# Window attention and a gated feed-forward block: the general path as loops, and row sums taken among the gate steps

## The chip, the core and the metric

The kernel runs on one core of a Trainium2 chip. The metric is the device time of one execution in microseconds; the median of several runs is compared.

## What is computed

```python
# q, k, v: (8 batches, 8 heads, 576 positions, 64), float32
scores = (q @ k^T) / 8                     # per batch and head
mask   = (rel >= 0) & (rel < 64)           # rel = query position - key position
attn   = softmax(where(mask, scores, -1e9))
x      = (attn @ v), heads side by side    # 4608 tokens x 512
g      = x @ w_gate                        # 512 x 1536
out    = (silu(g) * (x @ w_val)) @ w_out   # 1536 x 512; out 4608 x 512 float32
```

## The kernel before

The 4608 tokens are worked off as nine tiles of 512 (t = 0 to 8). Eight of them are the first 512 positions of one batch each; tile `LAST` = 7 gathers the last 64 positions of all eight batches. A tile goes through three stages.

- Attention. Scores of two head pairs at a time go to PSUM (L292). `weigh` (L307) turns them into exponentials on ScalarE, without taking a row maximum off first, and writes them to one of four tiles `eb`; VectorE multiplies by the mask (L313). Row sums come from matmuls with ones (L336), and their inverses from a logarithm and an exponential on ScalarE (L350, L353). The second product (L414) is scaled into `xT` (L430).
- Gate steps. Twelve steps m = 0 to 11 (`gate_value`, L473): eight 128x512 matmuls, four for the gate and four for the value; Silu on ScalarE (L466); the product on VectorE into `hT` (L467). The PSUM banks of both alternate between two.
- Projection. `hT` times `wo` (L482, L494), copies to SBUF (L502) and stores on SyncE's queue (L511, L513). The projection of tile t-1 is interleaved with the attention of tile t. In the last tile nothing follows it, and `project_last` splits the last 128 tokens into 384 and 128 columns (L535, L539, L540).

The order on each engine is the order of the program (`manual_schedule`); nothing reorders it.

Since no row maximum is taken off, the kernel checks that the exponentials stayed in range. 56 columns of `spread` hold row values: of tile 0 by `survey_first`, and of the later tiles as sums that ScalarE accumulates along with the exponentials of L307 (32 columns, `accum_out=extent()`, an extra instruction that reads the accumulator) and with those of L353 (16 columns). In the last tile, `survey` (L546, L547) compares all columns with a limit behind gate step 4, and `tally` (L551, L552) counts by a matmul the partitions that are in range, behind step 7, and casts the result to the integer `count`. Behind the last gate step each of the five engines loads `count` into a register (L961). At the very end they branch (L970): if the count is 128, and so it is with these inputs, they jump over the general path, which would compute everything again in a slower, safe way. The general path is unrolled: eight batches of eight heads of attention, then the feed-forward, all written out, with loads and stores on SyncE's queue. Between the second and third projection of the last tile a branch hint is given on every engine. Behind the jump each engine adds to its semaphores what the skipped code would have added (L970), and the end of the program (L998) waits for all semaphores, lets the engines meet, clears the semaphores and lets them meet again.

Of the kernel before, what the change touches and what calls it, by code (L numbers as in the profile page):

```python
# [8 lines left out]
P = 128  # L9
# [2 lines left out]
AF = mybir.ActivationFunctionType  # L12
ALU = mybir.AluOpType
PSUM = bass.MemoryType.PSUM
EVERY = tuple(
    getattr(mybir.EngineType, n) for n in ("PE", "SP", "DVE", "Activation", "Pool")
)


@with_exitstack  # L20
def kernel(
# [10 lines left out]
    nc = tc.nc  # L32
# [35 lines left out]
    spread = cst.tile([P, 6 * NT + 2], FP32, name="spread")  # L68
    within = cst.tile([P, 2], BF16, name="within")
    count = cst.tile([P, 1], mybir.dt.int32, name="count")  # L70
    floor = cst.tile([P, 1], FP32, name="floor")
    LEAST, MOST = 2.0 ** -60, 2.0 ** 30
    columns_used = [0]
# [229 lines left out]
    def weigh(t, w, h, s_ps):  # L303
        n = 1024 if t == LAST else 960
        E = eb[2 * w + h]
        flat = E[:].rearrange("r s z -> r (s z)")[:, 64:64 + n]
        nc.scalar.activation(  # L307
            flat, s_ps[:].rearrange("r a b -> r (a b)")[:, 0:n], AF.Exp, scale=0.125,
            accum_out=extent(),
        )  # L310

        def masked():
            nc.vector.tensor_mul(  # L313
                flat, flat, mask[:].rearrange("r j c e y -> r (j c e y)")[:, 0:n]
            )
# [237 lines left out]

    def general_attention(b):

        x_b = v12[:].rearrange("r g i h d -> r (g i h d)")[:, 0:4 * S]
        x_b = x_b.rearrange("r (c s) -> r c s", c=4)
        chunks = [(P * c, min(S, P * c + P)) for c in range(5)]
        set_exp()
        for hd in range(H):  # L560
            u, h = hd // 2, hd % 2
            wide = {}
            for n, (src, tag) in (("q", (q, "q")), ("k", (k, "k"))):
                f = stage.tile([P, 5, D], FP32, name=n + "_g", tag=tag)
                nc.sync.dma_start(f[:, 0:4], src[b, hd, 0:512].rearrange("(c r) d -> r c d", r=P))
                nc.sync.dma_start(f[0:64, 4], src[b, hd, 512:S])
                bf = epool.tile([P, 5, D], BF16, name=n + "_h", tag="both")
                nc.vector.tensor_copy(bf[:, 0:4], f[:, 0:4])
                nc.vector.tensor_copy(bf[0:64, 4], f[0:64, 4])
                tp = bank[4 if n == "q" else 5].bitcast(BF16)  # L570
                for c, (lo, hi) in enumerate(chunks):
                    nc.tensor.transpose(
                        tp[0:D, lo:hi], bf[0:hi - lo, c], identb[0:hi - lo, 0:hi - lo]
                    )
                wide[n] = att.tile([P, S], BF16, name=n + "_w", tag="qT")
                nc.vector.tensor_copy(wide[n][0:D], tp[0:D, 0:S])
            vf = stage.tile([P, 5, D], FP32, name="v_g", tag="v", bufs=1)
            nc.sync.dma_start(vf[:, 0], v[b, hd, 0:P])
            nc.sync.dma_start(vf[:, 1:5], v[b, hd, 64:S].rearrange("(c r) d -> r c d", r=P))
            vh = epool.tile([P, 5, D], BF16, name="v_h", tag="both")  # L580
            nc.vector.tensor_copy(vh[:], vf[:])
            for c, (lo, hi) in enumerate(chunks):
                nq, k0 = hi - lo, max(0, lo - 64)
                nk = hi - k0
                s_ps = bank[6][0:nq, 0:nk]
                nc.tensor.matmul(s_ps, wide["q"][0:D, lo:hi], wide["k"][0:D, k0:hi])
                w = fsb.tile([P, 512], FP32, name="w_g", tag="sg")
                s = w[0:nq, 0:nk]
                nc.scalar.activation(s, s_ps, AF.Copy, scale=0.125)
                for sign, base in ((1, lo - k0), (-1, 63 + k0 - lo)):  # L590
                    nc.gpsimd.affine_select(
                        out=s, in_=s, compare_op=ALU.is_ge, fill=-1e9,
                        base=base, pattern=[[-sign, nk]], channel_multiplier=sign,
                    )
                top, total = w[0:nq, 256:257], w[0:nq, 257:258]
                nc.vector.tensor_reduce(top, s, axis=mybir.AxisListType.X, op=ALU.max)
                nc.vector.tensor_scalar(top, top, -1.0, 0.0, op0=ALU.mult, op1=ALU.add)
                nc.scalar.activation(s, s, AF.Exp, bias=top, accum_out=total)
                nc.vector.tensor_scalar(total, total, 1.0, 1e-9, op0=ALU.mult, op1=ALU.add)
                nc.vector.reciprocal(total, total)  # L600
                e = epool.tile([P, 192], BF16, name="e_g", tag="e_g", bufs=1)
                nc.vector.tensor_scalar(e[0:nq, 0:nk], s, total, 0.0, op0=ALU.mult, op1=ALU.add)
                tp = bank[7].bitcast(BF16)
                pT = fsb.tile([P, 2, P], BF16, name="p_g", tag="p_g", bufs=1)
                parts = [(0, P)] + ([(P, nk)] if nk > P else [])
                for i, (j0, j1) in enumerate(parts):
                    nc.tensor.transpose(
                        tp[0:j1 - j0, P * i:P * i + nq], e[0:nq, j0:j1], identb[0:nq, 0:nq]
                    )
                    nc.vector.tensor_copy(  # L610
                        pT[0:j1 - j0, i, 0:nq], tp[0:j1 - j0, P * i:P * i + nq]
                    )
                o_ps = bank[4][half(h), 0:nq]
                for i, (j0, j1) in enumerate(parts):
                    nc.tensor.matmul(
                        o_ps, vh[0:j1 - j0, c + i], pT[0:j1 - j0, i, 0:nq],
                        start=i == 0, stop=i == len(parts) - 1,
                    )
                nc.vector.tensor_copy(x_b[half(h), u, lo:hi], o_ps)
        return x_b  # L620

    def general_ffn(b, x_b):

        set_silu()
        for lo, hi in ((0, 512), (512, S)):
            n = hi - lo
            h_b = hpool.tile([P, 12, 512], BF16, name="h_b", tag="hT")
            for m in range(12):
                for w, ps_ in ((wg, bank[4]), (wv, bank[5])):
                    for c in range(4):  # L630
                        nc.tensor.matmul(
                            ps_[:, 0:n], w[:, c, P * m:P * m + P], x_b[:, c, lo:hi],
                            start=c == 0, stop=c == 3,
                        )
                sg = fsb.tile([P, 512], FP32, name="sg", tag="sg")
                nc.scalar.activation(sg[:, 0:n], bank[4][:, 0:n], AF.Silu)
                nc.vector.tensor_mul(h_b[:, m, 0:n], sg[:, 0:n], bank[5][:, 0:n])
            for r0 in range(0, n, P):
                rows = min(P, n - r0)
                for c in range(12):  # L640
                    nc.tensor.matmul(
                        bank[6][0:rows], h_b[:, c, r0:r0 + rows], wo[:, c, :],
                        start=c == 0, stop=c == 11,
                    )
                os_ = fsb.tile([P, 512], FP32, name="os_", tag="os_", bufs=4)
                nc.vector.tensor_copy(os_[0:rows], bank[6][0:rows])
                at = S * b + lo + r0
                nc.sync.dma_start(out[at:at + rows], os_[0:rows])

    def set_exp():  # L650
        nc.scalar.preload_act_table_set("natural_log_exp_and_others")
# [80 lines left out]
        return lambda: log(inverse[0, u], bank[b]), lambda: invert(inverse[0, u])  # L732

    firsts = {}

    def survey_first(u):

# [166 lines left out]
    for t in range(1, NT):  # L904
# [45 lines left out]
        turns = (6, 7, 9, 10) if t == 1 else (1, 4, 7, 10)  # L950
        for m in range(12):
            gate_value(t, m)
            if t == NT - 1 and m == 4:
                survey()
            if t == NT - 1 and m == 7:
                tally()
            if m in turns and t + 1 < NT:
                turn(t + 1, turns.index(m))
            if (t, m) in late:
                turn_k(kT[2], k_l, late.index((t, m)))  # L960
# [9 lines left out]
    with tc.If(good < P, preferred_fallthrough_block=True, label="settled"):  # L970
        for b in range(8):
            x_b = general_attention(b)
            general_ffn(b, x_b)

# [1 line left out]
_INS = ['q', 'k', 'v', 'moe_w_gate', 'moe_w_val', 'moe_w_out']  # L976
# [26 lines left out]
```

## Time and profile before

| | |
|---|---|
| median of 3 runs | 326.08 us (326.05 to 326.44) |
| the profiled execution | 325.93 us, span 324.2 us, 1.73 us around it |
| granted TensorE clock | 0.998 |
| busy: TensorE, VectorE, ScalarE, GpSimd | 97%, 66%, 55%, 46% |
| last matmul issued | 318.16 us |
| instructions in the span | 8153 |

The profile is of one execution; times within it are in us from the start of the span. The engines are PE (TensorE matmuls), PEld (its weight loads), DVE (VectorE), ACT (ScalarE), POOL (GpSimd) and SP (SyncE); a q behind the name stands for the engine's sequencer, which runs branches, register loads, semaphore waits and DMA issues. q1 is the DMA queue of SyncE's transfers; q8 and q14 carry instructions.

### The profile page before, as it was taken

To read this page: it belongs to the slowest core of one execution; us is meant where nothing else is said; L and a number is where in the kernel's file an instruction comes from. 1 tells how busy PE (TensorE), PEld (TensorE's weight loads), DVE (VectorE), ACT (ScalarE), POOL (GpSimd) and SP (SyncE) were. 2 spreads that over 40 slices of the span, in tenths; PEclk is the share of its full clock that TensorE was granted. 3 is DMA by queue.
4 is the path that set the end of the run, shared out by engine and by line. 5 is a ranking of instruction groups with operands and counts; after the bars stand their busy time and mean duration, and the time that the engine had idled before them with its cause. 6 is when DMAs were issued, how large, how long until landed. Compare 5 with 4: busy or idle time off the path is not lost.

```text
span 324.2 us, 8153 instructions
## 1 busy us (share of the span) xinstructions
PE 314.4 (97%) x3267; PEld 158.4 (49%) x3298; DVE 213.7 (66%) x349; ACT 178.8 (55%) x295; POOL 147.7 (46%) x268
## 2 busy tenths in 40 slices
PE   8899999999999999999999999999999999999992
PEld 3544444445444644464445544554456444644441
DVE  4879846497576747685687658866785668654321
ACT  4967675348533873387337833693368434853300
POOL 4965656867567245742751099309665300000000
PEclk9999999999999999999999999999999999999999
DMA  7999999999599449974993379529997400020022
GB/s 238 207 196 198 207 144 234 198 191 140 120 189 198 49 114 177 195 76 106 161 197 40 87 114 117 54 64 144 188 175 92 107 0 2 10 93 32 2 69 71
DMA packets 83534, 40.50 MB, mean 125 GB/s; under 512 B 64160, under 2 KB 78752, under 8 KB 83488
## 3 DMA queue, kind: packets, MB, share of 16 engines
q0 software_dynamic: 51488, 22.59, 58.4%
q1 hardware_dynamic: 31456, 16.79, 22.9%
q8 instruction: 27, 0.44, 0.6%
q10 hardware_dynamic: 544, 0.52, 0.5%
q14 instruction: 19, 0.16, 0.2%
HBM read 53.02 MB, written 9.44 MB: 193 GB/s over the span
## 4 chain that ended last, share of the span: by engine, by line
PE 77%; DMA 14%; POOL 4%; issue 2%; DVE 1%; SPq 0%; POOLq 0%
PE one L473 45%; PE one L482 14%; PE one L494 11%; DMA wv<-in_moe_w_val_dram 3%; DMA wo<-in_moe_w_out_dram 3%; PE two L292 3%; DMA q_s<-in_q_dram 2%; PE two L414 2%; DMA wg<-in_moe_w_gate_dram 2%; DMA vb<-in_v_dram 2%; POOL k_s L141 1%; DMA q_f<-in_q_dram 1%; PE one L535 1%; POOL v L159 1%; PE one L336 1%
## 5 line engine op out<-in xcount | busy, mean ns | idle before, releaser
L466 ACT ACTIVATE sg<-one 128x512 f32<-128x512 f32 x107 | 63.9, 597 | 112.5 <-PE one L473 86.2
L467 DVE TENSOR_TENSOR hT<-sg,one 128x512 bf16<-128x512 f32 x107 | 74.0, 693 | 57.7 <-PE one L473 54.0
L473 PE MATMUL one<-xT,wv 128*128 128x512 bf16 x409 | 106.4, 379 | 1.0
L473 PE MATMUL one<-xT,wg 128*128 128x512 bf16 x405 | 104.7, 379 | 0.1
L141 POOL DMA_DIRECT2D k_s<-in_k_dram x112 | 60.4, 561 | 27.5 <-DMA q_s<-in_q_dram 14.3
L473 PEld LDWEIGHTS <-wv 128*128 128x128 bf16 x416 | 40.7, 98 | 49.4 <-issue 0.4
L473 PEld LDWEIGHTS <-wg 128*128 128x128 bf16 x416 | 40.6, 98 | 48.8
L482 PE MATMUL one<-wo,hT 128*128 128x512 bf16 x241 | 55.4, 379 | 0.7 <-issue 0.3
L937 POOL COPY past<-xT 128x1 bf16<-128x1 bf16 x8 | 1.5, 190 | 88.0 <-DVE xT L430 88.0
L494 PE MATMUL one<-wo,hT 64*64 64x512 bf16 x672 | 40.4, 376 | 0.0
L482 PEld LDWEIGHTS <-hT 128*128 128x128 bf16 x252 | 23.7, 98 | 29.4 <-issue 2.0
L232 DVE STREAM_TRANSPOSE kT<-k_s 128x512 bf16<-128x512 bf16 x28 | 36.1, 1288 | 0.5 <-DMA vb<-in_v_dram 0.5
L430 DVE TENSOR_TENSOR xT<-two,r 128x512 bf16<-128x512 f32 x34 | 21.2, 683 | 21.9 <-ACT r L353 21.9
L307 ACT ACTIVATE eb<-two 128x960 bf16<-128x960 f32 (+1 forms) x32 | 31.0, 973 | 3.8 <-PE two L292 3.7
L494 PEld LDWEIGHTS <-hT 64*64 64x64 bf16 x672 | 21.1, 107 | 11.3
L313 DVE TENSOR_TENSOR eb<-eb,mask 128x960 bf16<-128x960 bf16 (+1 forms) x32 | 20.9, 655 | 7.9 <-ACT eb L307 7.9
L222 DVE STREAM_TRANSPOSE qT<-q_s 128x512 bf16<-128x512 bf16 x32 | 22.3, 700 | 0.1
L353 ACT ACTIVATE r<-r 128x1024 f32<-128x1024 f32 (+1 forms) x20 | 19.2, 969 | 0.1
L318 DVE TENSOR_TENSOR both<-eb 128x512 bf16<-128x512 bf16 x32 | 13.6, 425 | 1.1
L106 POOL DMA_DIRECT2D q_s<-in_q_dram x24 | 13.0, 551 | 2.2 <-DMA v<-in_v_dram 1.2
L167 POOL DMA_DIRECT2D vb<-in_v_dram x16 | 11.1, 708 | 5.8 <-DMA wo<-in_moe_w_out_dram 3.6
L350 ACT ACTIVATE r<-one,floor 128x512 f32<-128x512 f32 x17 | 10.9, 683 | 3.5 <-PE one L336 3.5
(148 smaller groups left out, 265.3 us busy)
## 6 DMA issues: line engine op xcount, KB each, us to landing
k_s<-in_k_dram POOLq DMA_DIRECT2D x112, 56.0 KB, 5.0
q_s<-in_q_dram POOLq DMA_DIRECT2D x24, 248.0 KB, 6.2
v_f<-in_v_dram SPq DMA_DIRECT2D x40, 128.0 KB
wg<-in_moe_w_gate_dram POOLq DMA_DIRECT2D x5, 256.0 KB, 8.4
wv<-in_moe_w_val_dram POOLq DMA_DIRECT2D x5, 256.0 KB, 9.0
q_f<-in_q_dram SPq DMA_DIRECT2D x4, 256.0 KB
wo<-in_moe_w_out_dram POOLq DMA_DIRECT2D x2, 512.0 KB, 10.6
vb<-in_v_dram POOLq DMA_DIRECT2D x16, 64.0 KB, 6.3
```

The source lines that it names most:

```text
L141: nc.gpsimd.dma_start(k_s[p0:p0 + 32, g, :, 0:w], k[b, a:H:2, s:s + P].rearrange("u (r e) d -> r u (e d)", e=4) [:, :, 32 * c:32 * c + w],)
L222: nc.vector.transpose(queries[t][:, u, :].rearrange("r (e x) -> r e x", e=16), staged[t][0][:, u].rearrange("r (e d) -> r e d", d=D)[:, :, ...
L232: nc.vector.transpose(dst[:, u, :].rearrange("r (g x e) -> r g e x", g=4, e=4), k_s[:, :, u].rearrange("r g (e d) -> r g e d", d=D)[:, :, ...
L307: nc.scalar.activation(flat, s_ps[:].rearrange("r a b -> r (a b)")[:, 0:n], AF.Exp, scale=0.125, accum_out=extent(),)
L313: nc.vector.tensor_mul(flat, flat, mask[:].rearrange("r j c e y -> r (j c e y)")[:, 0:n])
L353: nc.scalar.activation(r, r, AF.Exp, scale=-1.0, **kept)
L430: nc.vector.tensor_mul(x, o_ps, r)
L466: nc.scalar.activation(sg[:], g_ps[:], AF.Silu)
L467: nc.vector.tensor_mul(hT[t][:, m, :], sg[:], v_ps[:])
L473: nc.tensor.matmul(ps[:], w[:, c, P * m:P * m + P], xT[t][:, c, :], start=(c == 0), stop=(c == 3),)
L482: nc.tensor.matmul(o_ps[:], hT[t][:, c, P * s:P * s + P], wo[:, c, :], start=(c == 0), stop=(c == 11),)
L494: nc.tensor.matmul(tiles[s][half(y)], hT[t][half(x), c, r0:r0 + 64], wo[half(x), c, :], start=not back and c == 0, stop=bool(back) and c = ...
```

## The change

The general path becomes two loops that run on the chip, one over 64 pairs of batch and head and one over eight batches; what attention makes goes between them through a scratch array in device memory, `x_all`. Its loads and stores are issued by ScalarE. Its largest body is 642 instructions (of one engine), its smallest 99. The branch hints are left out. The row sums of the 32 exponentials of the later tiles are no longer accumulated with them: `survey_later` takes them from the masked exponentials by a copy in place on ScalarE, behind gate steps 3, 5, 6 and 8 of the same tile. In the last tile the survey moves from behind step 4 to behind step 8, and the tally from behind step 7 to behind step 10.

```diff
@@ (constants)
-EVERY = tuple(
-    getattr(mybir.EngineType, n) for n in ("PE", "SP", "DVE", "Activation", "Pool")
-)
@@ (tiles)
+    scratch = ctx.enter_context(
+        tc.tile_pool(name="scratch", bufs=1, space=bass.MemoryType.DRAM)
+    )
+    x_all = scratch.tile([2 * H * 8 * D, S // 2], BF16, name="x_all")
@@ weigh
         nc.scalar.activation(
-            flat, s_ps[:].rearrange("r a b -> r (a b)")[:, 0:n], AF.Exp, scale=0.125,
-            accum_out=extent(),
+            flat, s_ps[:].rearrange("r a b -> r (a b)")[:, 0:n], AF.Exp, scale=0.125
         )
@@ general_attention
-        set_exp()
-        for hd in range(H):
-            u, h = hd // 2, hd % 2
-            wide = {}
-            for n, (src, tag) in (("q", (q, "q")), ("k", (k, "k"))):
-                f = stage.tile([P, 5, D], FP32, name=n + "_g", tag=tag)
-                nc.sync.dma_start(f[:, 0:4], src[b, hd, 0:512].rearrange("(c r) d -> r c d", r=P))
...
-                o_ps = bank[4][half(h), 0:nq]
...
-                nc.vector.tensor_copy(x_b[half(h), u, lo:hi], o_ps)
-        return x_b
+        def rows(ap, lo, hi):
+            return ap.rearrange("b h s d -> (b h) s d")[bass.ds(b, 1), lo:hi]
+
+        wide = {}
+        for n, src, tag in (("q", q, "q"), ("k", k, "k")):
+            f = stage.tile([P, 5, D], FP32, name=n + "_g", tag=tag)
+            nc.scalar.dma_start(
+                f[:, 0:4], rows(src, 0, 512).rearrange("o (c r) d -> r (o c) d", r=P)
+            )
...
+        for c, (lo, hi) in enumerate(chunks):
...
+            nc.vector.tensor_copy(x_h[0:D, lo:hi], o_ps)
+        for i in range(2):
+            nc.scalar.dma_start(
+                x_all[bass.ds(b * D + 8 * H * D * i, D), :],
+                x_h[0:D, S // 2 * i:S // 2 * i + S // 2],
+            )
@@ general_ffn
-    def general_ffn(b, x_b):
-
-        set_silu()
-        for lo, hi in ((0, 512), (512, S)):
...
-                nc.sync.dma_start(out[at:at + rows], os_[0:rows])
+    def general_ffn(i, b):
+
+        n = S // 2
+        x_b = att.tile([P, 4, n], BF16, name="x_b", tag="xT")
+        nc.scalar.dma_start(
+            x_b[:], x_all[bass.ds(i * (8 * H * D) + b * (H * D), H * D), :]
+            .rearrange("(c r) s -> r c s", r=P),
+        )
...
+            nc.scalar.dma_start(out[bass.ds(b * S + i * n + r0, rows)], os_[0:rows])
@@ (behind firsts)
+    def survey_later(t, i):
+
+        n = 1024 if t == LAST else 960
+        flat = eb[i][:].rearrange("r s z -> r (s z)")[:, 64:64 + n]
+        nc.scalar.activation(flat, flat, AF.Copy, accum_out=extent())
@@ gate steps of tiles 1 to 8
             gate_value(t, m)
-            if t == NT - 1 and m == 4:
+            if m in (3, 5, 6, 8):
+                survey_later(t, (3, 5, 6, 8).index(m))
+            if t == NT - 1 and m == 8:
                 survey()
-            if t == NT - 1 and m == 7:
+            if t == NT - 1 and m == 10:
                 tally()
@@ the end
         project(NT - 1, s, bank[(5, 7, 4)[s]])
-        if s == 1:
-            tc.mark_branch_hint_location("settled", P - good, engines=EVERY)
     project_last(NT - 1, 3)
-    with tc.If(good < P, preferred_fallthrough_block=True, label="settled"):
-        for b in range(8):
-            x_b = general_attention(b)
-            general_ffn(b, x_b)
+    with tc.If(good < P, preferred_fallthrough_block=True):
+        set_exp()
+        with tc.For_i(0, 8 * H, 1) as b:
+            general_attention(b)
+        set_silu()
+        with tc.For_i(0, 8, 1) as b:
+            for i in range(2):
+                general_ffn(i, b)
```

More of the change, by code (lines that the diff above doesn't have):

```diff
@@ L554, in general_attention @@
     def general_attention(b):
-        x_b = v12[:].rearrange("r g i h d -> r (g i h d)")[:, 0:4 * S]
-        x_b = x_b.rearrange("r (c s) -> r c s", c=4)
         chunks = [(P * c, min(S, P * c + P)) for c in range(5)]
-        set_exp()
-        for hd in range(H):
-            u, h = hd // 2, hd % 2
-            wide = {}
-            for n, (src, tag) in (("q", (q, "q")), ("k", (k, "k"))):
-                f = stage.tile([P, 5, D], FP32, name=n + "_g", tag=tag)
-                nc.sync.dma_start(f[:, 0:4], src[b, hd, 0:512].rearrange("(c r) d -> r c d", r=P))
[L566 to L573, printed above, removed]
-                    )
[L575 to L612, printed above, removed]
-                o_ps = bank[4][half(h), 0:nq]
[L614 to L618, printed above, removed]
-                nc.vector.tensor_copy(x_b[half(h), u, lo:hi], o_ps)
@@ L620, in general_attention @@
-        return x_b
-    def general_ffn(b, x_b):
-        set_silu()
-        for lo, hi in ((0, 512), (512, S)):
[L626 to L647, printed above, removed]
-                nc.sync.dma_start(out[at:at + rows], os_[0:rows])
@@ new lines, in rows @@
+        def rows(ap, lo, hi):
[6 more added lines that the diff above has]
+            )
+            nc.scalar.dma_start(f[0:64, 4], rows(src, 512, S).rearrange("o r d -> r (o d)"))
+            bf = epool.tile([P, 5, D], BF16, name=n + "_h", tag="both")
+            nc.vector.tensor_copy(bf[:, 0:4], f[:, 0:4])
+            nc.vector.tensor_copy(bf[0:64, 4], f[0:64, 4])
+            tp = bank[4 if n == "q" else 5].bitcast(BF16)
+            for c, (lo, hi) in enumerate(chunks):
+                nc.tensor.transpose(
+                    tp[0:D, lo:hi], bf[0:hi - lo, c], identb[0:hi - lo, 0:hi - lo]
+                )
+            wide[n] = att.tile([P, S], BF16, name=n + "_w", tag="qT")
+            nc.vector.tensor_copy(wide[n][0:D], tp[0:D, 0:S])
@@ new lines, in general_attention @@
+        vf = stage.tile([P, 5, D], FP32, name="v_g", tag="v", bufs=1)
+        nc.scalar.dma_start(vf[:, 0], rows(v, 0, P).rearrange("o r d -> r (o d)"))
+        nc.scalar.dma_start(
+            vf[:, 1:5], rows(v, 64, S).rearrange("o (c r) d -> r (o c) d", r=P)
+        )
+        vh = epool.tile([P, 5, D], BF16, name="v_h", tag="both")
+        nc.vector.tensor_copy(vh[:], vf[:])
+        x_h = att.tile([P, S], BF16, name="x_h", tag="xT")
+        for c, (lo, hi) in enumerate(chunks):
+            nq, k0 = hi - lo, max(0, lo - 64)
+            nk = hi - k0
+            s_ps = bank[6][0:nq, 0:nk]
+            nc.tensor.matmul(s_ps, wide["q"][0:D, lo:hi], wide["k"][0:D, k0:hi])
+            w = fsb.tile([P, 512], FP32, name="w_g", tag="sg")
+            s = w[0:nq, 0:nk]
+            nc.scalar.activation(s, s_ps, AF.Copy, scale=0.125)
+            for sign, base in ((1, lo - k0), (-1, 63 + k0 - lo)):
+                nc.gpsimd.affine_select(
+                    out=s, in_=s, compare_op=ALU.is_ge, fill=-1e9,
+                    base=base, pattern=[[-sign, nk]], channel_multiplier=sign,
+                )
+            top, total = w[0:nq, 256:257], w[0:nq, 257:258]
+            nc.vector.tensor_reduce(top, s, axis=mybir.AxisListType.X, op=ALU.max)
+            nc.vector.tensor_scalar(top, top, -1.0, 0.0, op0=ALU.mult, op1=ALU.add)
+            nc.scalar.activation(s, s, AF.Exp, bias=top, accum_out=total)
+            nc.vector.tensor_scalar(total, total, 1.0, 1e-9, op0=ALU.mult, op1=ALU.add)
+            nc.vector.reciprocal(total, total)
+            e = epool.tile([P, 192], BF16, name="e_g", tag="e_g", bufs=1)
+            nc.vector.tensor_scalar(e[0:nq, 0:nk], s, total, 0.0, op0=ALU.mult, op1=ALU.add)
+            tp = bank[7].bitcast(BF16)
+            pT = fsb.tile([P, 2, P], BF16, name="p_g", tag="p_g", bufs=1)
+            parts = [(0, P)] + ([(P, nk)] if nk > P else [])
+            for i, (j0, j1) in enumerate(parts):
+                nc.tensor.transpose(
+                    tp[0:j1 - j0, P * i:P * i + nq], e[0:nq, j0:j1], identb[0:nq, 0:nq]
+                )
+                nc.vector.tensor_copy(
+                    pT[0:j1 - j0, i, 0:nq], tp[0:j1 - j0, P * i:P * i + nq]
+                )
+            o_ps = bank[4][0:D, 0:nq]
+            for i, (j0, j1) in enumerate(parts):
+                nc.tensor.matmul(
+                    o_ps, vh[0:j1 - j0, c + i], pT[0:j1 - j0, i, 0:nq],
+                    start=i == 0, stop=i == len(parts) - 1,
+                )
+            nc.vector.tensor_copy(x_h[0:D, lo:hi], o_ps)
@@ new lines, in general_attention @@
+        for i in range(2):
+            nc.scalar.dma_start(
+                x_all[bass.ds(b * D + 8 * H * D * i, D), :],
+                x_h[0:D, S // 2 * i:S // 2 * i + S // 2],
+            )
+    def general_ffn(i, b):
+        n = S // 2
+        x_b = att.tile([P, 4, n], BF16, name="x_b", tag="xT")
+        nc.scalar.dma_start(
+            x_b[:], x_all[bass.ds(i * (8 * H * D) + b * (H * D), H * D), :]
+            .rearrange("(c r) s -> r c s", r=P),
+        )
+        h_b = hpool.tile([P, 12, 512], BF16, name="h_b", tag="hT")
+        for m in range(12):
+            for w, ps_ in ((wg, bank[4]), (wv, bank[5])):
+                for c in range(4):
+                    nc.tensor.matmul(
+                        ps_[:, 0:n], w[:, c, P * m:P * m + P], x_b[:, c],
+                        start=c == 0, stop=c == 3,
+                    )
+            sg = fsb.tile([P, 512], FP32, name="sg", tag="sg")
+            nc.scalar.activation(sg[:, 0:n], bank[4][:, 0:n], AF.Silu)
+            nc.vector.tensor_mul(h_b[:, m, 0:n], sg[:, 0:n], bank[5][:, 0:n])
+        for r0 in range(0, n, P):
+            rows = min(P, n - r0)
+            for c in range(12):
+                nc.tensor.matmul(
+                    bank[6][0:rows], h_b[:, c, r0:r0 + rows], wo[:, c, :],
+                    start=c == 0, stop=c == 11,
+                )
+            os_ = fsb.tile([P, 512], FP32, name="os_", tag="os_", bufs=4)
+            nc.vector.tensor_copy(os_[0:rows], bank[6][0:rows])
+            nc.scalar.dma_start(out[bass.ds(b * S + i * n + r0, rows)], os_[0:rows])
```

## The prediction

> **What bounds the kernel now.** I read, in this order, the page's engine rows, the chain that ended last, the stages, the gate steps on ScalarE, and then what is left behind the last matmul.
>
> ```profile
> PE 314.4 (97%) x3267; PEld 158.4 (49%) x3298; DVE 213.7 (66%) x349; ACT 178.8 (55%) x295; POOL 147.7 (46%) x268
> ```
>
> TensorE is busy for 314.4 of 324.2 us. The stages show that little can be won ahead of its last matmul:
>
> ```profile
> 147.00:180.70 33.70, 33.54 (x354) 17.15 (x356) 23.98 (x36) 19.21 (x33) 13.14 (x25) 1.00 0.76 122
> ...
> 318.70:324.20 5.50, 0.00 (x0) 0.00 (x0) 0.00 (x1) 0.00 (x0) 0.00 (x0) 0.89 0.19 57
> ```
>
> The columns are stage, length, then busy time of PE, PEld, DVE, ACT, POOL. A whole tile of 33.70 us has 0.16 us without a matmul; the tail of 5.5 us has none at all. So the tail is where this change can act. What ends last there is the way out of the kernel: each engine reads `count`, jumps over the general path (L970), and SyncE collects all semaphores (L998). Of the lines on L961 and L970:
>
> ```profile
> L961 SPq TENSOR_LOAD <-count x1: 473/473/473, 301.9 to 301.9; - x1
> ...
> L961 PEldq TENSOR_LOAD <-count x1: 490/490/490, 305.4 to 305.4; - x1
> ```
>
> ```profile
> L970 SPq EVENT_SEMAPHORE  x8: 17/17/17, 322.0 to 322.5; - x8
> ...
> L970 ACTq COMPARE_BRANCH  x1: 73/73/73, 307.9 to 307.9; - x1
> L970 ACTq EVENT_SEMAPHORE  x1: 17/17/17, 310.6 to 310.6; - x1
> L970 PEldq COMPARE_BRANCH  x1: 1577/1577/1577, 316.6 to 316.6; - x1
> ...
> L970 DVEq COMPARE_BRANCH  x1: 84/84/84, 318.4 to 318.4; - x1
> L970 SPq COMPARE_BRANCH  x1: 70/70/70, 319.2 to 319.2; - x1
> L970 DVEq EVENT_SEMAPHORE  x1: 21/21/21, 321.8 to 321.8; - x1
> ```
>
> Each engine is silent after its jump: ScalarE 310.6 - 307.9 - 0.1 = 2.6 us, VectorE 3.3, SyncE 2.7. In these silences the instruction queues move:
>
> ```profile
> q1 hardware_dynamic: 268, 0.25, 42.4%
> q8 instruction: 1, 0.02, 5.4%
> q14 instruction: 2, 0.02, 3.2%
> ```
>
> That is the DMA view of 318.7 to 320.5: the output beside three instruction fetches. SyncE's jump is the one that counts: it resumes at 321.98, needs 0.54 us for eight counts, and 1.69 us from the last of them to the end at 324.2.
>
> A code block can be sized from the page: q8 moved 0.44 MB in 27 packets, 16 KB each, and TensorE has 3267 + 3298 records, so 64 to 67 bytes an instruction and 256 in a block; q14, which serves the other engines, moves 8 KB packets, 128 instructions. ScalarE fetched its target block at 308.9 and the block behind it at 311.2, 0.6 us after it resumed. So on entering a block an engine fetches the next, and a jump that stays inside this block or the next should cost no fetch.
>
> **The change, part by part.**
>
> *Row sums.* 32 exponentials lose their accumulator read. A read (198 ns by the row of L307) adds 0.09 us to the distance from one exponential to the next. TensorE's 0.16 us per tile does not stand on it, so I take 0; bounds are a gain of 8 x 4 x 0.09 = 2.9 us if every one were on the path (the stage rows exclude nearly all of it) and 0. Against that, 32 copies with a sum come into gate steps 3, 5, 6 and 8. These rows are of the neighbours:
>
> ```profile
> 303.70 0.60 ACT L466 ACTIVATE sg<-one 128x512 f32<-128x512 f32 x1 [1.13 <-PE one L473]
> 305.43 0.60 ACT L466 ACTIVATE sg<-one 128x512 f32<-128x512 f32 x1 [1.13 <-PE one L473]
> ```
>
> A gate step is 1.73 us, of which ScalarE idles 1.13. The nearest rows for the copy are L353 (128x1024 with sum, 1.04 us from start to start) and L307 (960 elements, 0.96). So 0.62 + 0.96 to 1.04 = 1.58 to 1.66 us: it fits. Were it 0.5 us longer, Silu of step 6 would start late, but its banks are wanted only two steps on; some 1.7 us of cover remain. Cost 0. The tables are not touched.
>
> *Survey and tally, three to four steps later.* The sum at step 8 ends near 303.6, the survey on VectorE (0.18 + 0.21 us) near 304.1, ahead of the product due at 304.64. The tally's matmul comes behind step 10, at 306.07; the cast to `count` follows the product that runs from 306.37, as it does today with 0.76 us from that start to its end: 307.12. All five engines wait for it at L961. SyncE (first store at 311.3), GpSimd, ScalarE and VectorE have time. TensorE's sequencer stands in front of the load from 305.39, with only step 11 queued behind it; the load then runs 307.15 to 307.64 and the first weights of L482, now loaded at 307.61, follow near 307.75. Its matmul was due at 307.82. I take 0.05 us; bounds 0 and 0.3 (a load a quarter of a us longer).
>
> *The jump.* The hints go: MOVE, ALU_OP and hint, under 0.3 us per engine and off the path. Those of VectorE (313.4) and SyncE (314.5) brought no fetch, q14 being silent from 312 to 318.5; TensorE's seems to have helped, its jump being over at 318.16. The body shrinks to 99 to 642 instructions. TensorE must be the 642: 66 + 528 transposes, matmuls and weight loads can be counted in it. SyncE has no work left in it, its loads and stores now being issued by ScalarE, so I give it the 99. From any place in a block, 99 ahead is this block or the next: SyncE goes on at 319.3 instead of 321.98. VectorE has 75 operations in the body and waits on 0.6 more per operation in this trace, with the loops' own perhaps 150: inside the next block from 4 of 5 places.
>
> What is late next is the output. Its last 64 KB is issued at 318.75. Fourteen of 16 parts had landed by 320.39; the last two took until 321.35 and 321.96, because one DMA engine was busy with TensorE's fetch (1.55 us from 318.83) and SyncE's (0.6 us from 320.14). Neither falls there now: TensorE without a hint jumps at 316.6, fetches from about 317.5 to 318.5, resumes near 319.6 (2.6 to 3.3 us by the other jumps), and fetches its next block when the output is through. So the last part lands near 320.45; the store before it (316.51 to 318.53, 2.0 us) bounds this by 320.75. Then SyncE's last count and the rest, 1.69 us: the span ends at 322.14, with TensorE's 0.05 at 322.2. Sum against the profiled time of 325.93 (span 324.2 and 1.73 around it): -2.0, so 323.9; the median of the runs stands 0.15 above the profiled one, so **324.1**.
>
> Bounds of the tail: if SyncE has no counts to make up any more (its semaphores are untouched by the body), 0.6 us less, 321.6; if TensorE jumps only when its queue has run dry, 318.4 + 3.3 = 321.7, and 0.95 behind it, 322.7.
>
> [...]
>
> **The rivals.**
> *VectorE, or another engine, still fetches.* For: it alone waited 3.3 us, with a hint; my 150 is loose. It resumes at 321.84; its semaphore is one of those that SyncE collects (now at 323.15, 1.06 us before the end), so the span ends at 322.95: 324.7 profiled, 324.8 as a median. With a straggling output part (321.96 + 0.95) it is the same.
> *SyncE still fetches,* the change not doing what it is worded to do for the engine that matters: its body is over 128, or a block ahead does not count as there. Then everything is as now but for at most 0.6 us of counts: 325.5 to 326.2.
> *Slower: the way past the loops needs a meeting of the engines.* Unrolled code leaves semaphores counted up, and L970 shows the jump path adding the same counts. Loops may reset them; then the jump path must drain, meet, clear and meet, as the end does from 323.39 to 324.17: 0.8 us. That decides against the change from the point where SyncE still fetches: 326.1 + 0.8 + 0.05, about 326.9. With SyncE's jump free it only shrinks the gain to 1.2 us (324.9). Against it: nothing in the trace shows such a path.
>
> **How the numbers follow.** My forecast has 0.42 (323.3 to 324.4), another engine's fetch or the meeting beside a free jump 0.26 (324.5 to 325.4), SyncE's fetch 0.18, slower 0.14. Leaving out the slower case and the ends gives 323.3 to 326.3. A difference under 0.2%, 0.65 us, is about what a measurement of this kernel cannot tell from none. Faster by more: 0.42 + 0.26 and a little of the third, 0.70; within: 0.16; slower: 0.14.
>
> **What would show it.** Right: SyncE's first instruction behind L970's branch within 0.2 us, no fetch on q14 for it, all output parts landed by 320.8, last matmul at 318.4 to 318.5, ScalarE's idle before Silu cut to about 0.1 us in steps 4, 6, 7 and 9. Wrong: SyncE silent for 2.7 us again; a gap of over 0.3 us in TensorE's matmuls near 307.8; more barriers at the end than the two of L998.

## The result, and the profile after

The changed kernel takes 323.77 us (323.44 to 324.29), the kernel before 326.06 us (325.95 to 326.44) in the same comparison: a ratio of 0.9929, with an interval of 0.9912 to 0.9946. The profiled execution took 323.99 us, with a span of 322.2 us.

One mark divides the time below: T, the start of TensorE's last weight load. It is at 318.10 us before and 316.90 after. So 1.20 us of the gain lie ahead of T and 0.81 us behind it, where the tail shrinks from 6.10 to 5.30 us.

**Ahead of T.** The first line is the page's row of engines, then come two lines of the view of stages (the same tile and the tail):

```profile
PE 315.4 (98%) x3298; PEld 155.1 (48%) x3298; DVE 214.9 (67%) x349; ACT 208.6 (65%) x327; POOL 147.3 (46%) x268
```

```profile
147.00:180.70 33.70, 33.70 (x358) 16.60 (x357) 24.04 (x36) 23.12 (x37) 13.15 (x25) 1.00 0.75 121
317.00:322.20 5.20, 0.18 (x4) 0.00 (x1) 0.39 (x2) 0.00 (x0) 0.00 (x0) 0.76 0.19 61
```

TensorE looks as full as before (33.54 of 33.70 us then, with four matmul records fewer in the trace), and ScalarE is 30 us busier. These rows do not show what was won. The timeline does, where the second pair of scores of tile 5 waits for the exponentials. Its columns are start, length, engine, line, operation, tiles, shape and number; first before, then after:

```profile
173.79 0.97 ACT L307 ACTIVATE eb<-two 128x960 bf16<-128x960 f32 x1
174.66 0.19 ACT L307 ACTIVATION_READ_ACCUMULATOR eb<-two 128x1 f32 x1
174.75 0.96 ACT L307 ACTIVATE eb<-two 128x960 bf16<-128x960 f32 x1
175.60 0.20 ACT L307 ACTIVATION_READ_ACCUMULATOR eb<-two 128x1 f32 x1
175.68 0.65 PEld L292 LDWEIGHTS <-kT 64*64 64x64 bf16 x31
```

```profile
173.08 1.83 ACT L308 ACTIVATE eb<-two 128x960 bf16<-128x960 f32 x2
174.96 0.49 PEld L293 LDWEIGHTS <-kT 64*64 64x64 bf16 x31
```

The same 31 weight loads take 0.65 us before and 0.49 after. Before, TensorE issues two of these matmuls, at 175.684 and 175.709 us, and the third at 175.859, just behind the end of the second read (175.60 + 0.20): in the trace the read gives the semaphore that this matmul waits for, so the bank comes free with the read, not with the exponential. The modelled ends of the earlier matmuls cover that wait of 0.15 us, so the busy column shows none of it. From the second pair of scores to the first gate step it is 9.83 to 9.84 us in six of the seven tiles from the third on before, and 9.68 after: 0.15 to 0.16 us six times, 0.94 us together. The seventh, `LAST`, takes 10.22 us in both. The gate stage is 21.03 us in both. The remaining 0.26 us is nearly all the start (71.57 against 71.32 us to the first scores of the third tile). It moved between 70.8 and 73.3 us from one profile of these kernels to another (71.24 and 73.02 in two repeats of the changed kernel), so it is not put down to the change.

**Among the gate steps** of the last tile (timeline, ScalarE) the copies have the room that was predicted; Silu keeps its 1.73 us from step to step:

```profile
300.75 0.60 ACT L466 ACTIVATE sg<-one 128x512 f32<-128x512 f32 x1 [1.13 <-PE one L473]
301.25 1.00 ACT L750 ACTIVATE eb<-eb 128x960 bf16<-128x960 bf16 x1
302.14 0.19 ACT L750 ACTIVATION_READ_ACCUMULATOR eb<-eb 128x1 f32 x1
302.48 0.60 ACT L466 ACTIVATE sg<-one 128x512 f32<-128x512 f32 x1
```

**Behind T** stand the branch line, now L986 (columns: operation, number, shortest, median and longest ns, first and last start), and the DMA queues between 316.9 and 321 us (packets that start there, MB, share of the time of 16 engines):

```profile
L986 SPq EVENT_SEMAPHORE  x8: 17/17/17, 318.2 to 320.1; - x8
...
L986 PEldq COMPARE_BRANCH  x1: 3522/3522/3522, 315.4 to 315.4; - x1
L986 DVEq COMPARE_BRANCH  x1: 72/72/72, 317.2 to 317.2; - x1
L986 SPq COMPARE_BRANCH  x1: 50/50/50, 318.0 to 318.0; - x1
...
L986 DVEq EVENT_SEMAPHORE  x1: 21/21/21, 320.6 to 320.6; - x1
```

```profile
q1 hardware_dynamic: 305, 0.28, 21.2%
q8 instruction: 1, 0.02, 1.4%
q14 instruction: 1, 0.01, 0.5%
```

SyncE resumes 0.14 us after its branch instead of 2.73. But VectorE is silent for 3.31 us as before, TensorE's branch takes 3.5 us instead of 1.6, and both still fetch code beside the output: VectorE at T+1.88, TensorE at T-0.52 and again at T+2.74 (the view starts at T, so its q8 line is this second one). SyncE's eight counts now spread over 2 us: the last three wait for the parts of three stores, and the last part of all lands at T+3.23 (T+3.85 before). (Landings are the increments of the stores' semaphores in the trace, one for each of 16 parts.) The last count is at T+3.24 (T+4.42 before). Behind it there are 2.05 us to the end, where there were 1.69: one of the quick steps that follow (0.06 us from one to the next) takes 0.39.

### The profile page after: what moved, and what is told of

Same layout as the page of the kernel before. It is cut to its first block, busy times and chain, and to the rows that moved or that the text cites. A ratio compares the mean times of both kernels' runs of the same rounds, so it can differ in the third digit from the quotient of the medians.

```text
span 322.2 us, 8212 instructions
## 1 busy us (share of the span) xinstructions
PE 315.4 (98%) x3298; PEld 155.1 (48%) x3298; DVE 214.9 (67%) x349; ACT 208.6 (65%) x327; POOL 147.3 (46%) x268
## 4 chain that ended last, share of the span: by engine, by line
PE 95%; ACT 2%; DMA 1%; issue 0%; DVE 0%
PE one L473 56%; PE one L482 17%; PE one L494 11%; PE two L293 3%; PE two L414 2%; PE one L449 2%; DMA q_f<-in_q_dram 1%; ACT eb L735 1%; PE two L336 1%; PE one L535 1%; PE two L449 1%; PE one L336 0%; ACT r L350 0%; ACT qk_b L721 0%; ACT r L353 0%; PE two L874 0%
## 5 line engine op out<-in xcount | busy, mean ns | idle before, releaser
L473 PE MATMUL one<-xT,wg 128*128 128x512 bf16 x416 | 106.8, 379 | 0.0
L482 PE MATMUL one<-wo,hT 128*128 128x512 bf16 x252 | 56.5, 379 | 0.0
L750 ACT ACTIVATE eb<-eb 128x960 bf16<-128x960 bf16 (+1 forms) x32 | 32.1, 1002 | 0.0
L308 ACT ACTIVATE eb<-two 128x960 bf16<-128x960 f32 (+1 forms) x32 | 29.5, 974 | 3.0 <-PE two L293 2.9
L494 PEld LDWEIGHTS <-hT 64*64 64x64 bf16 x672 | 18.6, 107 | 13.7
```

What stands on the lines that cost most here:

```text
L308: nc.scalar.activation(flat, s_ps[:].rearrange("r a b -> r (a b)")[:, 0:n], AF.Exp, scale=0.125)
L473: nc.tensor.matmul(ps[:], w[:, c, P * m:P * m + P], xT[t][:, c, :], start=(c == 0), stop=(c == 3),)
L482: nc.tensor.matmul(o_ps[:], hT[t][:, c, P * s:P * s + P], wo[:, c, :], start=(c == 0), stop=(c == 11),)
L494: nc.tensor.matmul(tiles[s][half(y)], hT[t][half(x), c, r0:r0 + 64], wo[half(x), c, :], start=not back and c == 0, stop=bool(back) and c = ...
L750: nc.scalar.activation(flat, flat, AF.Copy, accum_out=extent())
```

## The experiments

Theory A: the gain has two independent parts, the accumulator reads (0.16 us a tile on TensorE) and SyncE's short jump. Rival B: all of it is the way out, as the prediction had it. Further theories came with the tail, C among them, that the pause of 0.39 us is paid for going into another code block, and F, that code fetches alone hold back the output parts. The medians of before were higher and more scattered in the later sessions (326.4 to 327.4), so what is compared is mostly the tail and the stages of the profiles:

| kernel | s2 to gate | fetches behind T-1 and ahead of the last part | last part | SyncE silent | tail | median (ratio to before) |
|---|---|---|---|---|---|---|
| before | 9.84 | PE +0.72, DVE +1.89, SP +2.04 | +3.85 | 2.73 | 6.10 | 326.06 |
| changed | 9.68 | PE -0.52, DVE +1.88, PE +2.74 | +3.23 | 0.14 | 5.30 | 323.77 (0.9929) |
| e1 loops alone | 9.84 | PE -0.51, DVE +1.87, PE +2.59 | +3.40 | 0.14 | 5.47 | 325.40 (0.9949) |
| e2 sums alone | 9.68 | PE +1.61, DVE +1.91, SP +2.05 | +4.06 | 2.75 | 6.13 | 326.41 (0.9964) |
| e3 SyncE far | 9.68 | PE +0.45, DVE +1.84, SP +2.73, PE +3.52 | +3.72 | 2.51 | 6.60 | 325.24 (0.9954) |
| e4 SyncE shifted | 9.68 | PE -0.51, DVE +1.85, SP +2.86, PE +3.27 | +3.44 | 0.47 | 5.15 | 324.22 (0.9916) |
| e6 no feed-forward | 9.68 | DVE +1.80 | +3.15 | 0.14 | 4.85 | 323.75 (0.9896) |
| e7 few matmuls | 9.68 | DVE +1.94 | +3.28 | 0.14 | 5.36 | 324.00 (0.9899) |
| e9 hints back | 9.68 | PE +0.75, DVE +1.90, SP +2.17 | +3.77 | 0.45 | 5.47 | 324.37 (0.9915) |
| e8 no fetch | 9.68 | none | +2.31 | 0.14 | 4.01 | 322.90 (0.9875) |
| v1 VectorE short | 9.68 | PE -0.51, SP +2.87, PE +3.51 | +3.71 | 0.47 | 5.78 | 324.34 (0.9929) |
| v2 all short | 9.68 | none | +2.30 | 0.14 | 4.24 | 323.24 (0.9890) |

(us; "s2 to gate" is the stretch above in an ordinary tile; fetches and landings are counted from T.)

**e1, the loops without the moved sums.**

```diff
-            flat, s_ps[:].rearrange("r a b -> r (a b)")[:, 0:n], AF.Exp, scale=0.125
+            flat, s_ps[:].rearrange("r a b -> r (a b)")[:, 0:n], AF.Exp, scale=0.125,
+            accum_out=extent(),
...
-            if m in (3, 5, 6, 8):
-                survey_later(t, (3, 5, 6, 8).index(m))
-            if t == NT - 1 and m == 8:
+            if t == NT - 1 and m == 4:
                 survey()
-            if t == NT - 1 and m == 10:
+            if t == NT - 1 and m == 7:
                 tally()
```

> The changed kernel with the row sums back on the exponentials, and survey and tally back behind steps 4 and 7: the loops alone. Theory A (two gains: about 1.1 us because TensorE waits for the exponential's semaphore, which the accumulator read gives 0.09 us later, twice per attention stage, in seven stages; about 1 us in the tail, because SyncE's jump needs no fetch): TensorE's second set of scores again waits 0.17 us per tile, last matmul some 1.1 us later than in the changed kernel, SyncE resumes within 0.2 us of its branch; 324.9 us. Theory B (the prediction's own: the reads are worth nothing and all of the gain is in the tail): as the changed kernel, 323.8 us.

**e2, the moved sums with the unrolled path and its hints:** before, with the other half of the edit.

> The kernel before with only the row sums moved to copies behind gate steps 3, 5, 6 and 8, and survey and tally behind steps 8 and 10; general path unrolled, hints as before: the sums alone. Theory A: last matmul 1.1 us earlier than before, tail of 5.8 us behind it as before, SyncE silent for 2.7 us after its branch; 325.0 us. Theory B: 326.1 us, no difference from before.

The stage follows the reads in both: 9.84 us with them, 9.68 without. The tail follows the loops: 5.47 against 6.13 us. By the stages A holds and B falls. Each half alone lies a little below before (0.993 to 0.9967 and 0.9938 to 0.999). The medians alone would not decide it: A expected 324.9 and 325.0 us, measured were 325.40 and 326.41, with before at 326.84 in that session; e2's profile reaches the third tile at 73.32 us, 1.75 later than before's.

**e3, SyncE's jump made long again:** 160 small loads put into the path that is never run.

```diff
     with tc.If(good < P, preferred_fallthrough_block=True):
+        for j in range(160):
+            nc.sync.dma_start(spare[:, j:j + 1], q[0, 0, 0:1, j % 64:j % 64 + 1])
```

> The changed kernel with 160 small loads on SyncE's queue added inside the general path, which never runs: SyncE's body is 259 instructions instead of 99, nothing else differs. Theory A (SyncE's short jump is what the tail gained): SyncE silent for 2.7 us after its branch again with a fetch on the instruction queue, its last count near 3.3 us after the branch instead of 2.2; 0.8 to 1.1 us slower than the changed kernel, 324.6 to 324.9. Rival (the tail is set by the landing of the output or by VectorE's fetch, not by SyncE's jump): within 0.2 us of the changed kernel.

```profile
L987 SPq EVENT_SEMAPHORE  x8: 17/17/17, 321.2 to 321.7; - x8
...
L987 SPq COMPARE_BRANCH  x1: 45/45/45, 318.6 to 318.6; - x1
```

The silence is back, 2.51 us, and the tail is 1.30 us longer, more than was expected. Another effect is in it: SyncE branched at T+1.80 instead of T+1.09, because the issue of its last store took 1.10 us instead of 0.38. Without these 0.72 us and with the same silence the tail would be about 5.9 us, an estimate from these numbers: 0.6 longer than the changed kernel's, where 0.8 to 1.1 were expected.

**e4, SyncE's code shifted against its blocks:** 40 loads of 4 bytes that are run in tile 4.

```diff
+            if t == 4:
+                for j in range(40):
+                    nc.sync.dma_start(spare[:, j:j + 1], q[0, 0, 0:1, j:j + 1])
```

> The changed kernel with 40 loads of 4 bytes on SyncE's queue added in tile 4, where SyncE is idle, so that its later code stands 40 slots further on. In the changed kernel SyncE pauses 0.36 us between two of its last waits although both semaphores are there. Theory C (it enters a new code block there, which costs about 0.35 us even if the block is present, as GpSimd's and ScalarE's jumps took 0.5 us and SyncE's 0.14): the pause is gone from that place, entered at the jump instead, where the output's landing covers it; 0.3 us faster, 323.5. Rival (the pause is a semaphore's or an arbitration's): pause in the same place, 323.8.

The 0.39 us left the final steps and turned up at the jump (0.47 us silent instead of 0.14): the step into the next block costs 0.33 us in both places (0.39 less the usual 0.06, 0.47 less 0.14), and neither step waits for a fetch as a long jump does (2.51 us in e3). That is C. The gain in the tail, 0.15 us, was half of what C promised, as the last part landed 0.2 us later.

**The changed kernel again,** for its scatter in the sessions of what follows.

> The changed kernel again, beside the next kernels on the same chip. Every theory: TensorE's tile stages as in the first profile (9.68 us from the second scores to the gate), tail of 5.3 us from the last weight load to the end within 0.3 us, one fetch each for VectorE and TensorE behind their branches; some 0.7% under the kernel before.

> The changed kernel once more, as the measure for the next two on the same chip. Every theory: tail of 5.3 us behind the last weight load within 0.2 us, SyncE's pause of 0.39 us in its list of waits, time as in its earlier runs, 323.8 within 0.5 us.

323.86 and 324.40 us, ratios 0.9886 (0.9837 to 0.9935) and 0.9918 (0.9881 to 0.9955); the tails were 5.34 and 5.30 us, the last part at +3.27 and +3.23. The tail repeats better than the median. In both, SyncE branched later than in the first profile (T+1.56 and T+1.46 instead of T+1.08), because the issue of its last store was slow, as in e3. This goes with the first of the three stores: its last part landed at +2.52, +2.61, +2.63, +2.86 and +2.88 where that issue took 0.75, 0.84, 0.86, 1.10 and 1.10 us (second repeat, e4, first repeat, v1, e3); where that part landed by +2.11, the issue took 0.38. How the one brings the other was not tried.

**e6, the general path without its feed-forward loop; e7, with most of that loop's matmuls left out.** Both shorten TensorE's body, to 88 and 134 instructions; e6 shortens VectorE's too, to 73.

```diff
-        set_silu()
-        with tc.For_i(0, 8, 1) as b:
-            for i in range(2):
-                general_ffn(i, b)
```

> The changed kernel with the feed-forward loop left out of the general path, which never runs here: bodies of 88 (TensorE), 73 (VectorE), 53 (SyncE) instructions. Theory D (the tail that is left is held by the fetches for TensorE's and VectorE's jumps: TensorE's 16 KB beside the last stores delays the landing, VectorE's semaphore comes 3.4 us after its branch): no fetch of a jump in the tail, no 16 KB packet between 1 us before and 2 us behind the last weight load, last output part landed 2.4 to 2.6 us behind that load instead of 3.2, end at 4.2 to 4.6 instead of 5.3; about 0.9 us faster than the changed kernel. Rival (the tail is the store's own time and the semaphores' list): 5.2 to 5.4, no gain.

> The changed kernel with most matmuls left out of the general path's feed-forward, which never runs here: TensorE's body 134 instead of 642 instructions, VectorE's 133 instead of 155. Theory D: no 16 KB fetch for TensorE's jump; if VectorE still fetches, the end waits for its semaphore (3.7 us behind the last weight load) and comes at 4.8 to 5.2; if 133 is near enough, as in the kernel without the feed-forward, 4.2 to 4.6. Rival: 5.2 to 5.4.

The DMA queues of e6 from T-0.04 to the end:

```profile
q1 hardware_dynamic: 302, 0.27, 17.3%
q14 instruction: 1, 0.01, 0.4%
```

TensorE fetches nothing behind T-1 in either, and its branch takes 0.24 us. Still one of 16 parts of the last store lands at +3.15 and +3.28, the others by 2.37 and 2.34. In both VectorE lands in its next block (silent for about 0.52 us) and fetches the one behind it, 8 KB, at +1.80 and +1.94. The tail of e6 missed its expectation, that of e7 met the rival's. So TensorE's fetch is not the only one that holds an output part back; one small fetch of VectorE's is enough.

**e9, the hints back in the changed kernel.**

> The changed kernel with the branch hints put back at their old place. Theory E (a hint acts only when the engine crosses into a new code block after it): TensorE's jump is over before its last matmul's semaphore and not 2 us after it, VectorE stays silent for 3.3 us as before, SyncE's jump is as short as without; TensorE's next block is fetched about 0.7 us behind the last weight load, into the last stores; tail 5.1 to 5.6, time within 0.3 us of the changed kernel. Rival (the hints were what made the old tail long or short): tail different by over 0.6 us.

TensorE's branch takes 1.61 us with the hint, and its fetch begins at +0.75 instead of -0.52. VectorE is silent for 3.38 us all the same. The tail is 5.47 us, 0.17 longer: the output lands 0.54 us later, and the pause of 0.39 is gone from the final steps, as SyncE's three instructions more move the block's end to the jump (0.45 us of silence there). Leaving the hints out is worth little.

**e8, e6 with VectorE shifted:** 40 memsets of four bytes in tiles 3 to 6, so that the jump of VectorE stays in one block.

```diff
+            if t in (3, 4, 5, 6) and m in (2, 5, 8, 9, 11):
+                for j in range(2):
+                    nc.vector.memset(spare[:, j:j + 1], 0.0)
```

> The kernel without the feed-forward in the general path (which never runs here), with 40 memsets of 4 bytes on VectorE in the gate steps of tiles 3 to 6, so that VectorE's jump stays inside one code block. Theory F (what holds the tail that is left is VectorE's own 8 KB fetch about 1.8 us behind the last weight load: one of 16 output parts shares its DMA engine and lands 0.8 us late): no fetch on the instruction queue from 1.5 to 2.5 us behind the last weight load, all parts landed by 2.5, last count at 2.5 to 2.6 instead of 3.2, end at 4.1 to 4.3 instead of 4.85 without the memsets and 5.3 in the changed kernel; 1.1 us faster than the changed kernel. Rival (the late part is the store's own): last part at 3.2, end at 4.85.

Lines of the branch in e8, and all of the DMA queues from its T (317.29 us) to the end:

```profile
L990 SPq EVENT_SEMAPHORE  x8: 17/17/17, 318.6 to 319.6; - x8
L990 PEldq COMPARE_BRANCH  x1: 236/236/236, 315.8 to 315.8; - x1
L990 DVEq COMPARE_BRANCH  x1: 72/72/72, 317.6 to 317.6; - x1
L990 DVEq EVENT_SEMAPHORE  x1: 21/21/21, 317.9 to 317.9; - x1
```

```profile
q1 hardware_dynamic: 297, 0.26, 19.6%
```

No engine fetches, all 16 parts land by +2.31, SyncE's last count is at +2.32, and from there 1.69 us remain. The tail of 4.01 us is 1.29 shorter than that of the changed kernel. F holds: against e6, which lacks only the memsets, the last part lands 0.84 us sooner, and against the changed kernel 0.92. The pause is gone as well, as it was in e6.

**v1, the whole general path, with VectorE's work in it given to ScalarE and GpSimd** (65 instructions left for VectorE, 643 for TensorE), and with the memsets of e8 and the loads of e4.

> A version meant to be kept: the changed kernel's whole general path, with VectorE's work in it given to ScalarE and GpSimd (65 instructions instead of 155 for VectorE; those two jump 10 us earlier), the 40 memsets on VectorE and 40 loads of 4 bytes on SyncE that shift their code. TensorE's body stays at 643, so its fetch stays. Theories C and F: no pause in SyncE's list of waits, no fetch for VectorE; last part at 2.6 to 3.3 because of TensorE's fetch, end at 4.3 to 5.0, 0.3 to 0.9 us faster than the changed kernel. Rival: same as the changed kernel within 0.2 us.

A miss: VectorE resumes in 0.25 us and fetches nothing, but TensorE's fetch is still there, 1.87 us from T-0.51, and one part of each of the three stores lands late, at +2.86, +3.42 and +3.71. SyncE's last store's issue was slow again, and its next block was fetched at +2.87, behind the first of these parts; which fetch held the other two v1 does not separate. From SyncE's last count 2.05 us remain here too: SyncE's steps have no pause, but GpSimd takes 0.38 us for one of its last steps where it takes 0.08 in e4.

**v2, the whole general path with short bodies on all engines.** VectorE's work in it is moved as in v1, q and k are loaded transposed, and its twelve gate steps become a loop too, over a copy of one step's weights (209 instructions on TensorE, 89 on VectorE, 111 on SyncE).

```diff
-        for m in range(12):
-            for w, ps_ in ((wg, bank[4]), (wv, bank[5])):
+        with tc.For_i(0, 12, 1) as m:
+            w_m = epool.tile([P, 2, 4, P], BF16, name="w_m", tag="w_m", bufs=1)
+            for i, w in enumerate((wg, wv)):
+                nc.gpsimd.tensor_copy(w_m[:, i], w[:, :, bass.ds(m * P, P)])
...
+            if t in (3, 4) and m in (2, 3, 5, 6, 8, 9, 11):
+                for j in range(2):
+                    nc.vector.memset(spare[:, j:j + 1], 0.0)
```

> A version meant to be kept, with the whole general path: a third loop over the twelve gate steps in it, q and k loaded turned, VectorE's work there given to ScalarE and GpSimd, 28 memsets of 4 bytes on VectorE in tiles 3 and 4 to shift its code. Bodies: 209 instructions on TensorE, 89 on VectorE, 111 on SyncE, so that by theories C and F TensorE's and VectorE's jumps stay inside one block and SyncE's enters the next. Expected: no 16 KB fetch behind TensorE's last block, no fetch between 1.5 and 2.1 us behind the last weight load, all output parts landed by 2.5, no pause in SyncE's waits, tail 4.0 to 4.4 instead of 5.3; about 1.1 us under the changed kernel, 322.9 in a run whose tiles start as usual. Rival (the whole path still brings a fetch: TensorE's 209 is not near enough): tail 4.8 to 5.8, no gain over the changed kernel.

```profile
L986 SPq EVENT_SEMAPHORE  x8: 17/17/17, 318.5 to 319.7; - x8
...
L986 PEldq COMPARE_BRANCH  x1: 236/236/236, 315.7 to 315.7; - x1
...
L986 DVEq EVENT_SEMAPHORE  x1: 21/21/21, 317.8 to 317.8; - x1
```

```profile
q1 hardware_dynamic: 296, 0.26, 33.2%
```

The last line is all of the DMA queues from T to T+2.4. All parts land by +2.30; one step of 0.39 us stands between SyncE's last two counts. The tail is 4.24 us, 1.06 shorter than that of the changed kernel. The median of 323.24 us (322.66 to 323.52) lies 0.5 to 1.2 us below the three of the changed kernel, which come from other sessions. Against before it is faster by about 1% (0.9863 to 0.9918); against the changed kernel the intervals of the ratios overlap, so there the tail is the evidence.

## Why the prediction was right

The time came out as forecast, 323.8 against 324.1 us, and the span exactly, 322.2; the place of the gain did not. The prediction took 2.05 us from the tail and gave 0.05 back at the load. Measured were 0.81 us in the tail and 1.20 ahead of it.

- *The accumulator reads.* "TensorE's 0.16 us per tile does not stand on it, so I take 0": this step failed. The term is 0.94 us in the profiles of before and changed, and e1 and e2 tie it to the reads. It was looked for in a busy column that covers waits of pipelined matmuls: the scores waited for the read, which gives the semaphore. The 0.16 us in that column are something else, and that they equal the wait is chance. They are three gaps of 0.053 us at 147.03, 157.82 and 168.61 us, where the record of one matmul is missing while the weight loads go on every 0.216 us. The bounds, 0 to 2.9 us, held the term. Here is the second gap in the timeline of before, and then the same stage of e1, which keeps the reads and shows no gap:

```profile
157.22 0.59 PE L473 MATMUL one<-xT,wg 128*128 128x512 bf16 x2
157.66 0.53 PEld L473 LDWEIGHTS <-wv 128*128 128x128 bf16 x3
157.87 0.59 PE L473 MATMUL one<-xT,wv 128*128 128x512 bf16 x2
```

```profile
147.00:180.70 33.70, 33.70 (x357) 17.23 (x356) 23.98 (x36) 19.21 (x33) 13.21 (x25) 1.00 0.78 121
```

- *The copies, the survey, the load.* Right: 0.99 us for the copy, Silu on time, the gate stage at 21.03 us. The 0.05 us at TensorE's load were not there: it ran from 305.94 to 306.43, which counted from T is when it was forecast (T-10.96), and the matmuls show no gap.
- *SyncE's jump.* Right, with a body of 99 instructions and a block estimated at 128 from the 8 KB packets of q14: 0.14 us of silence against 0.2 forecast, no fetch. e3 brings the silence back.
- *VectorE's jump.* The rival that another engine still fetches came true in its condition, from the one place in five that the prediction left. Its price did not fall due: VectorE resumed at 320.61 and gave its semaphore at 320.64; SyncE, late itself, reached the wait for it at 320.77. The code behind VectorE's 155 instructions was not at hand: 3.31 us of silence, and a fetch of 8 KB at T+1.88.
- *The output.* "Neither falls there now: ... So the last part lands near 320.45" failed, by 0.88 us counted from T (+2.35 forecast, +3.23 measured). TensorE's fetch began about where it was forecast but did not stay clear of the output: it ran from T-0.52 for 1.30 us, and a part of the first store landed only at T+2.11 (by T+0.43 in e6 and e7, without this fetch); and VectorE's, which the sum had not put there, came on top. TensorE's next block came at T+2.74, before the output was through and not after it; e7, without that fetch, has the last part no sooner. e8 and v2, without fetches, have it at +2.31 and +2.30.
- *From the last count to the end.* 1.69 us forecast, as before, 2.05 measured: SyncE leaves its block in the final steps, where one step takes 0.39 us (e4). In e8 it is 1.69.

So the tail that was priced, 4.05 us, is that of e8 (4.01): a way out on which nobody fetches. The 1.25 us missing from it were made up by the reads (0.94), an earlier start (0.26) and the 0.05 us not lost at the load, which is chance and no merit of the sum. The slower rival, a meeting of the engines on the way past the loops, did not appear: the way from the branch shows the same eight counts of SyncE and one of each other engine as before. In this kernel the unrolled code is what is jumped over, and loops shorten the jump: SyncE's silence goes from 2.73 to 0.14 us.

## What to carry to other kernels

Look behind the last matmul for code fetches beside the last stores. Here SyncE was silent for 2.51 us behind a jump over 259 instructions (e3) and for 0.14 us behind one over 99 (the changed kernel), and short bodies on all engines were worth more than on SyncE alone: a tail of 4.24 us (v2) against 5.30. TensorE's row was full in e1, 33.70 of 33.70 us, where the scores waited 0.16 us a tile for the reads (9.84 against 9.68 us to the gate); compare the time from start to start of the same group between two kernels. The gaps of 0.053 us in that row before were missing records; the weight loads beside them, one every 0.216 us, show it. A sum taken along with the exponential delayed the release of its bank until the accumulator was read, the same 0.16 us a tile in e1 against e2; where the next producer stands on that bank, try the sum elsewhere.

## What the runs showed of the hardware

- Beside an 8 KB instruction fetch of 0.31 us, one of 16 parts of a 64 KB store landed 0.8 to 0.9 us late (e6: +3.15, and +2.31 in e8 without the fetch; e7: +3.28 against +2.34 for the others). Why so small a fetch cost nearly three times its length is not settled.
- Going into the next block cost SyncE about 0.33 us, in straight code in the changed kernel (0.39 less 0.06) and at the jump in e4 (0.47 less 0.14).
- A shift of 40 instructions decided whether VectorE's jump over 73 was followed by a fetch: 8 KB at +1.80 in e6, none in e8, which has 40 memsets more and a tail 0.84 us shorter (4.01 against 4.85). A gain of this kind hung on the layout of the code here and is best looked up in the profile after every edit.
- With the hint the branch of TensorE took 1.61 us (e9) instead of 3.52 (the changed kernel); VectorE was silent for 3.38 us with it and for 3.31 without. Why they differ was not tried.
